# Turning the second unit's wide loads without a regrouping copy, first loads from two queues, a small mask pattern, and a new order

## The chip, the core and the metric

The kernel runs on one core of one Trainium2 chip. The metric is the device time of one execution in microseconds (us). Three executions of the kernel before took 289.61, 290.24 and 291.42 us; the median is 290.24. Engines are named as in the profile: PE is TensorE, ACT is ScalarE, DVE is VectorE, POOL is GpSimd, SP is SyncE. SP only issues transfers here.

## What is computed

Chunk-selected causal attention on 4 batches, 8 heads, 768 positions of 64 elements, followed by a gated feed-forward layer on 3072 tokens of 512 elements with a hidden width of 1536. All inputs and the output are fp32.

```python
k_chunks = k.reshape(B, H, nc, chunk, D)            # nc = 24 chunks of 32 keys
k_min, k_max = k_chunks.min(axis=3), k_chunks.max(axis=3)
ub = sum over d of max(q * k_min, q * k_max)        # an upper bound per query and chunk
top_chunks = argsort(where(causal, ub, -1e9))[..., -6:]
scores = where(chunk in top_chunks and causal, q @ k.T / sqrt(D), -1e9)
x = softmax(scores) @ v                             # heads side by side: 3072 x 512
return (sigmoid(x @ w_gate) * (x @ w_val)) @ w_out
```

## The kernel before

The 3072 tokens are cut into eight units, u0 to u7, of 384 tokens or less: three blocks of 128 positions each. u0 holds the first blocks of batches 0, 1 and 2, in which every causal key is selected (at most four chunks), so that it needs no choice. u1 holds blocks 1 to 3 of batch 0, u2 blocks 4 and 5 of batch 0 and the first block of batch 3, and so on. Each unit is attended, and then goes through the feed-forward layer; u4 with u5 and u6 with u7 go through it in pairs, with seven block products in place of eight.

Every piece of work is added to a plan with `plan.add` (lines 49 to 72): a name, the engines that may do it, what it reads and writes. The order of all pieces, the engine of each and the slot of each buffer are written out in the string `ORDER` (lines 94 to 254): `kn_u1_3@POOL:1` means that the piece `kn_u1_3` goes to POOL and its new buffer takes slot 1 of its kind. The first engine in a piece's list is taken where `ORDER` names none. Each engine, and each queue of transfers, runs its pieces strictly in that order.

The names that matter here:

- `kf0_b`, `kf1_b`, `qf0_b`, `qf1_b`, `vf_b` (lines 514 to 528): the loads of u0 for batch b; k and q in two halves of 4 heads, each 128 x 4 rows of 256 bytes (512 rows), v in one load of 1024 such rows. They are issued on SP.
- `k0_u1` to `k3_u1`, `q0_u1` to `q3_u1` (`load_wide`, lines 530 to 539): the wide loads of u1, two heads each, 256 rows of 768 bytes; those of u2 are 256 rows of 512 bytes. In them one partition holds three consecutive positions (x) of each head. They are issued on SP.
- `kn_u1_p`, `qn_u1_p` (`turned`, lines 684 to 698): a copy [128, 384] fp32 on ACT, DVE or POOL that brings the two heads of one position side by side. Then `kT_u1_p`, `qT_u1_p`: three PE transpositions of 128 x 128 fp32 through `ident32` into PSUM.
- `kt_`, `hk0_`, `hk1_`, `kx0_`, `kx1_`, `kcr_` for keys, `qf_`, `qm_`, `hq0_`, `hq1_` for queries: casts, reductions and copies of what was turned. `ub_u1` are the bound products, which need all four `qf_u1`, all four `qm_u1` and `kcr_u1`. `ubn`, `mx`, `ap`, `apt`, `hqm` make the choice from them.
- for u0 and each batch b: `kfT_b`, `qfT_b` (transpositions), `kf16_b`, `qf16_b` (casts), `scm_b` (the causal mask, added by a product), `scf_b` (scores), `expf_b_e`, `pvf_b_e`, `rzf_b_e`, `xf_b_e`, `xpsf_b_e`, `xTf_b_e`. When the last `xTf` is done, `g_u0_0` starts, the first product of the feed-forward layer (line 940).
- `epat0` and `epat` (lines 454 to 462): a mask pattern [64, 2, 24, 32] in fp16, cleared by DVE and filled on POOL by two selections of 32 x 768. `hkp...` (line 476) copy it eight times to the upper or lower halves of the key tiles.
- `ident` (POOL) and `ident16` (DVE, its fp16 cast); `wm_0` to `wm_23` are 24 products without use, which keep PE busy.
- `wg0`, `wv0` to `wg2`, `wv2`, `wo0` to `wo2`: the weights, issued by POOL, which converts them to fp16 on the way. `wg0` and `wv0` come behind `after0` and the others behind `after1` (lines 493 to 511): copies of one word on POOL that wait for the load of `qf1_1` and of `qf1_2`.

ACT runs no transfers before. Its first instruction is the load of the activation table, its second `kn_u1_1`.

Of the kernel before, what the change touches and what calls it, by code (L numbers as in the profile page):

```python
# [94 lines left out]
k3_u1:0 epat0:0 k1_u1 tri0 epat k0_u1 q1_u1 q3_u1 q2_u2:1 hkp100@POOL kf1_0:0 qf0_0:1 kn_u1_1:0 kf0_0 hkp111@ACT ident  # L95
qf1_1:2 hkp010@POOL ident16 hkp011 wm_0:0 k2_u1 kT_u1_1:1 q3_u2 kn_u1_3@POOL:1 wm_1 q2_u1 kt_u1_1:0 wm_2 kcr0
qn_u1_3:2 k2_u2 qn_u1_1@DVE:3 v10 qf1_0 qT_u1_3:2 kx0_u1_1 vf_0:3 hkp110 wm_3 after0 qf_u1_3:0 qf0_1 kx1_u1_1:0 wm_4
tri kn_u1_0:4 kn_u1_2@POOL:5 wm_5 qn_u2_3@DVE:6 kT_u1_0:3 wm_6 kf0_1:4 kT_u1_3:4 kt_u1_0:1 kx1_u1_0 wm_7 q1_u2
qm_u1_3@ACT:0 kfT_0:5 kx1_u1_3 kf1_1 wm_8 hk0_u1_0 wm_9 kxf0 vf_1:5 hkp101 q0_u2 v16_0_0 kf16_0@DVE:0 qf1_2:0
hk0_u1_1@POOL kx0_u1_0 qfT_0:6 wm_10 wm_11 qf16_0:2 wm_12 scm_0:7,2 kt_u1_3:2 wm_13 scf_0:1 kT_u1_2:1 kn_u2_2@POOL:4  # L100
kx0_u1_3 kf0_2:1 expf_0_1:2 wm_14 kT_u2_2:6 kxf1:1 kf1_2 expf_0_0 scm_1:3,4 q0_u1 hkp001 qn_u2_1:1 qT_u1_1:2 hq0_u1_3
pvf_0_1:5 qf0_2 rzf_0_1:0 kcr_f qf_u1_1@DVE kfT_1:7 k3_u2 kf16_1:2 qT_u2_1:2 vf_2:3 hq1_u1_3 after1 pvf_0_0:7
hk1_u1_0@POOL wm_15 k0_u2 rzf_0_0:1 qm_u1_1@ACT kx1_u2_2:1 wg0 qf_u2_1:1 kx0_u1_2 qfT_1:2 kx1_u1_2 wv0 k1_u2 wm_16
xf_0_0:0 v_0_3:4 qf16_1:5 hk1_u1_3 qn_u1_2@POOL:4 v_0_1:2 qn_u1_0@DVE:3 kt_u1_2:1 scf_1:3 kfT_2:7 vf1_2:1 expf_1_0
kx0_u2_2 vf1_1:2 qT_u1_2:2 vc_1 hq1 kf16_2:5 qT_u1_0:1 ap0 wm_17 wv1 xf_0_1:1 qf_u1_2 pvf_1_0:3 qfT_2:7 qf_u1_0@DVE
expf_1_1:1 v_0_2:1 scm_2:5,2 ap1 qm_u1_2@ACT qm_u1_0@POOL wm_18 qf16_2@DVE:4 hk1_u1_1@ACT pvf_1_1:1 wm_19 kcr_u1@POOL
xpsf_0_0:4,0 qn_u2_0:3 rzf_1_1:0 wm_20 kn_u2_3@POOL:2 xf_1_1:2 scf_2:2 hkf1 kt_u2_2@DVE:0 xpsf_1_1:7 expf_2_1:3
xpsf_0_1:1 rzf_1_0:0 xf_1_0:0 hq0_u1_2@POOL hq0_u1_0 ub_u1:6,2 kcr1 wg1 xTf_0_0@ACT vc_2@ACT qn_u2_2@POOL:4 hkp000@ACT
kn_u2_0@DVE:5 wg2 pvf_2_1:3 wm_21 rzf_2_1:0 qT_u2_3:4 xTf_1_1 wm_22 ubn0_u1:0 hq1_u1_0@POOL xf_2_1:2 expf_2_0 ubm0_u1
wv2 qf_u2_3@DVE hkf0@ACT pvf_2_0:7 qT_u2_0:6 hq1_u1_1@POOL rzf_2_0:0 xpsf_1_0:3 xTf_0_1@ACT xpsf_2_1:4 xf_2_0:1 wm_23  # L110
xTf_1_0@ACT hk0_u1_2@POOL qT_u2_2:0 hq0 kn_u2_1:0 ubn1_u1 wo1 xTf_2_1@ACT xpsf_2_0:5 xTf_2_0 kT_u2_3:1 k10_1:0
mx0_u1:0 g_u0_0:7,0,0 hk1_u1_2@POOL ap0_u1 wo0 v_u0_0:3 ubm1_u1 kt_u2_3@DVE:1 apt0_u1:0 g_u0_1:2,1,1 hq1_u2_1@POOL
hqm0_u1_2@ACT hqm0_u1_0 v_u0_1:4 tanh_u0_1 g_u0_2:5,2,2 hk0_u1_3@POOL tanh_u0_0 hg_u0_1 qm_u2_3@POOL:0 qf_u2_2
sc_u1_3_0:2,1 hg_u0_0 tanh_u0_2 sc_u1_0_0:7,3 sc_u1_3_1:4 qf_u2_0 v_u0_2:0 hq1_u1_2@DVE exp_u1_0_0 kx1_u2_3 kT_u2_1:5
qm_u2_0@ACT sc_u1_0_1:3 kT_u2_0:6 kx0_u2_1 exp_u1_0_1 sc_u1_3_2:7 mx1_u1 exp_u1_3_2 g_u0_3:3,3,3 exp_u1_3_0
hq0_u2_1@DVE sc_u1_2_0:7,0 hq0_u2_0@DVE cm_u1_3 v_0_4:5 tanh_u0_3 v_u0_3:2 kx0_u2_3 exp_u1_3_1 hg_u0_2 hq0_u1_1@POOL
sc_u1_2_1:3 exp_u1_2_0 g_u0_4:1,1,4 kx1_u2_1 v16_0_3 hk1_u2_3@ACT hg_u0_3 v_u0_4:4 ap1_u1 tanh_u0_4 g_u0_5:0,0,5
hg_u0_4 v_u0_5:7 apt1_u1 tanh_u0_5 kx0_u2_0 hqm1_u1_2 exp_u1_2_1 sc_u1_2_2:2 hqm1_u1_0@DVE sc_u1_1_0:1,2 g_u0_6:4,2,6
cm_u1_0 hq0_u2_2@DVE sc_u1_1_1:0 v_u0_6:3 tanh_u0_6 v11 exp_u1_1_0 kx1_u2_0 g_u0_7:4,3,7 hq1_u2_3@POOL hg_u0_6
kt_u2_1:2 qm_u2_1@ACT cm_u1_1 v_u0_7:1 hg_u0_5 hq1_u2_0@POOL kcr_u2 sc_u1_0_2:5 wo2 exp_u1_0_2 sc_u1_1_2:3  # L120
g_u0_8:7,1,8 exp_u1_1_2 hq0_u2_3 v16_0_1 v_u0_8:5 exp_u1_1_1 cm_u1_2 tanh_u0_8 g_u0_9:3,2,9 hk1_u2_1@POOL qm_u2_2@ACT
tanh_u0_7 v_u0_9:0 exp_u1_2_2 hg_u0_7 g_u0_10:7,0,10 hk0_u2_1 ub_u2:4,2 tanh_u0_10 kt_u2_0:2 hk1_u2_2@ACT v_u0_10:1
tanh_u0_9 g_u0_11:7,3,11 v16_0_2 hg_u0_10 v_u0_11:6 ubn0_u2:0 tanh_u0_11 k11_1 hg_u0_8 pv_u1_3:3 hg_u0_9 pv_u1_1:1
pv_u1_2 hg_u0_11 sc_u1_7_1:4,1 sc_u1_7_2:7 rz_u1_1:0 pv_u1_0 sc_u1_4_1:5,3 rz_u1_0:1 exp_u1_4_1 sc_u1_5_1:0,2
o0_u0_0:6,0 x_u1_0:0 exp_u1_5_1 mx0_u2:0 exp_u1_7_1 sc_u1_4_2:5 sc_u1_4_0:1 ubn1_u2 exp_u1_4_0 sc_u1_7_0:0 k01_1
ap0_u2 x_u1_1:2 exp_u1_7_0 sc_u1_6_1:4,0 o1_u0_0 apt0_u2:0 exp_u1_4_2 xps_u1_0:2,1 cm_u1_7 mx1_u2 xps_u1_1:1
exp_u1_7_2 sc_u1_6_2:3 xT_u1_0@ACT sc_u1_5_0:0 cm_u1_4 hk1_u2_0 exp_u1_5_0 sc_u1_5_2:5 o2_u0_0 hqm0_u2_0 exp_u1_6_1
o0_u0_1:7,1 hqm0_u2_2@ACT cm_u1_5 osb_u0_0@DVE vf1_3:6 exp_u1_5_2 ap1_u2 sc_u1_6_0:2 out_u0_0 hk0_u2_3@ACT hk0_u2_2
pv_u1_4:0 pv_u1_5 exp_u1_6_0 sc_u2_3_0:4,3 rz_u1_2:0 sc_u2_3_1:6 apt1_u2 o1_u0_1 k00_1 x_u1_2:1 exp_u2_3_1 hqm1_u2_2
q00_1:1 exp_u1_6_2 pv_u1_7:5 cm_u1_6 exp_u2_3_0 sc_u2_7_1:2,1 xps_u1_2:0 sc_u2_3_2:6 cm_u2_3 pv_u1_6 xT_u1_2  # L130
exp_u2_3_2 o2_u0_1 rz_u1_3:0 xT_u1_1@ACT x_u1_3:0 hqm1_u2_0@DVE sc_u2_7_0:3 o0_u0_2:4,0 hk0_u2_0 q10_1 xps_u1_3:0
o1_u0_2 xT_u1_3@ACT exp_u2_7_0 sc_u2_4_0:6,2 o2_u0_2 k16_1_0@ACT:1 kx0_1_1 k16_1_2:3 v_0_5:0 exp_u2_7_1 v16_0_4
g_u1_0:1,0,12 kx1_1_3:1 osb_u0_2 k16_1_3:4 v_u1_0:5 tanh_u1_0 kx0_1_2 exp_u2_4_0 g_u1_1:0,1,13 cm_u2_7 hq1_u2_2
kt_1_0:2 qf1_3:3 sc_u2_4_1:3 sc_u2_1_0:2,0 v_u1_1:4 q11_1 exp_u2_1_0 kt_1_3:0 q01_1 tanh_u1_1 g_u1_2:1,2,14 cm_u2_1
osb_u0_1 kt_1_2:5 sc_u2_1_2:6 sc_u2_7_2:2 v_u1_2:0 exp_u2_7_2 hk0_1_0@DVE tanh_u1_2 sc_u2_1_1:7 hg_u1_1 v16_0_5
g_u1_3:2,3,15 exp_u2_1_2 hg_u1_0 hk1_1_2@ACT cm_u2_4 v_u1_3:1 kx1_1_1 out_u0_2 exp_u2_1_1 g_u1_4:4,1,16 kx1_1_0
sc_u2_4_2:6 pv_u2_1:5 tanh_u1_4 v_u1_4:7 kx0_1_3 exp_u2_4_2 k16_1_1@ACT:1 out_u0_1 hg_u1_2 g_u1_5:4,0,17 tanh_u1_3
v_1_1:4 v_u1_5:6 kx1_1_2 tanh_u1_5 kf1_3:2 exp_u2_4_1 g_u1_6:0,2,1 qf0_3 hg_u1_4 v_u1_6:2 hg_u1_3 tanh_u1_6 kx0_1_0
pv_u2_3:4 g_u1_7:3,1,0 hg_u1_6 k01_2:0 sc_u2_2_2:7,3 sc_u2_0_0:1,0 qf0_u4_0:0 v_u1_7:0 v_1_0:1 kcr_1 exp_u2_0_0
qf0_u3_1:1 sc_u2_2_0:2 tanh_u1_7 qf0_u3_0 g_u1_8:1,3,2 v16_1_1 exp_u2_2_2 qf0_u3_2 exp_u2_2_0 sc_u2_2_1:3 hg_u1_5  # L140
v_u1_8:7 qm_u3_0@ACT:0 cm_u2_2 qf0_u3_3 g_u1_9:2,2,3 k00_2 cm_u2_0 tanh_u1_8 qf0_u4_2 hg_u1_7 sc_u2_0_1:6 k11_2
tanh_u1_9 v_u1_9:1 hg_u1_8 exp_u2_2_1 sc_u2_0_2:0 qm_u3_2 g_u1_10:2,0,4 hq0_u3_0@ACT kt_1_1:3 pv_u2_2 exp_u2_0_1
v_u1_10:7 qf0_u4_3 exp_u2_0_2 v16_1_0 hk0_1_1@DVE ub_u3:3,6 tanh_u1_10 k10_2 hk1_1_1 hk0_1_3@ACT sc_u2_6_1:0,3
hq0_u3_2@POOL ubn1_u3:0 pv_u2_0 g_u1_11:2,1,6 rz_u2_1:0 ubn0_u3 hk1_1_3 vf_3:5 rz_u2_0:1 qf0_u4_1 v_u1_11:6 tanh_u1_11
# [5 lines left out]
x_u2_2:0 hqm0_u3_2@ACT rz_u2_3:0 kx0_2_3 cm_u3_1 qfT_3:5 v16_1_3 kfT_3:1 x_u2_3:1 q11_2 qf16_3:5 hq1_u3_0@POOL  # L150
sc_u3_6_0:0,2 xT_u2_0 sc_u3_0_0:4,0 exp_u3_1_2 xps_u2_3:3 o2_u1_1 kf16_3:3 xT_u2_3 v16_1_2 kx1_2_3:1 exp_u3_0_0
xps_u2_2:2 sc_u3_0_2:5 cm_u3_0 xT_u2_2@ACT kt_2_2:0 exp_u3_6_0 scf_3:7,3,3 o0_u1_2:1,0 q00_2 exp_u3_0_2 kx1_2_2
sc_u3_0_1:4 expf_3_0 pv_u3_1:2 xps_u2_1:0 o1_u1_2 expf_3_1:1 cmf_3_0 kx0_2_0 exp_u3_0_1 cmf_3_1 pvf_3_0:5 xT_u2_1@ACT
# [142 lines left out]
def kernel(  # L296
# [159 lines left out]
    def pattern(e):  # L456
        for i in range(2):
            t = at(epat)[32 * i:32 * i + 32, i]
            nc.gpsimd.affine_select(out=t, in_=t, compare_op=ALU.not_equal, fill=NEG, base=0,
                                    pattern=[[-1, NC], [0, CH]], channel_multiplier=1)  # L460
# [776 lines left out]
```

## Time and profile before

| | |
|---|---|
| Median of three runs | 290.24 us (289.61 to 291.42) |
| The profiled execution's own time | 291.67 us |
| Its span, first to last instruction | 290.0 us |
| First matmul (`wm_0`) | starts at 7.50 us |
| `g_u0_0`, the first feed-forward product | starts at 34.40 us |
| PE busy before / from 34.4 us on | 22.75 of 34.40 us / 251.3 of 255.6 us |
| First-loads: bytes (u0, u1, u2) | 2.36 + 1.57 + 1.05 MB |

All times below are us from the span's start. "Busy" on PE counts a matmul from its start to the modelled end; matmuls overlap. PEclk is the granted TensorE clock as a share of full speed. In the DMA views, q1 is the queue of transfers issued by SP, q0 that of POOL; a row gives packets, MB, and the time that the packets took as a share of the 16 DMA engines' time. MB are counted at the destination.

### The profile page before, as it was taken

What the parts mean: (1) busy time and instruction counts of PE and PEld (TensorE: products, weight loads), DVE (VectorE), ACT (ScalarE), POOL (GpSimd) and SP (SyncE); (2) the same over time, 40 slices, a digit from 0 to 9 for tenths busy, and PEclk for the clock granted to TensorE, in tenths of its full rate; (3) what the DMA queues carried; (4) which work ended last, traced back from release to release, by engine and by line L of the source; (5) the groups of instructions that cost most, each with busy time, mean ns of one, the idle gap of its engine ahead of it and who ended that gap; (6) DMA issues with size and microseconds to landing.
All of it is one profiled execution on the core that took longest, in us unless ns stands there. A gap on an engine that the chain in (4) does not pass through costs nothing.

```text
span 290.0 us, 7126 instructions
## 1 busy us (share of the span) xinstructions
PE 274.1 (95%) x2650; PEld 174.3 (60%) x2650; DVE 233.0 (80%) x642; ACT 215.2 (74%) x457; POOL 112.4 (39%) x180
## 2 busy tenths in 40 slices
PE   0979799999999999999999999999999999999994
...
GB/s 185 239 242 185 204 203 192 157 157 184 217 177 171 212 181 167 219 203 193 175 40 1 3 38 38 73 5 0 0 3 0 75 72 38 36 1 2 1 106 113
DMA packets 123379, 32.71 MB, mean 113 GB/s; under 512 B 111440, under 2 KB 120400, under 8 KB 123344
## 3 DMA queue, kind: packets, MB, share of 16 engines
...
HBM read 30.67 MB, written 6.29 MB: 127 GB/s over the span
## 4 chain that ended last, share of the span: by engine, by line
PE 82%; ACT 10%; DVE 4%; POOL 1%; issue 1%; ACTq 0%; POOLq 0%; DVEq 0%
PE o_u L971 21%; PE sc_u L857 11%; PE g_u L940 10%; PE v_u L940 10%; PE pv_u L890 7%; PE ube_u L796 2%; PE sug_u6u L1049 2%; PE suv_u6u L1049 2%; ACT gate_u4u L1074 2%; PE suv_u4u L1049 2%; PE xps_u L917 1%; PE srg_u6u L1049 1%; PE sug_u4u L1049 1%; PE spare L1136 1%; PE srv_u6u L1049 1%
## 5 line engine op out<-in xcount | busy, mean ns | idle before, releaser
L868 ACT ACTIVATE att_u<-sc_u 128x512 f16<-128x512 f32 (+3 forms) x184 | 91.4, 554 | 15.3 <-PE sc_u L857 14.6
L874 POOL TENSOR_SCALAR_AFFINE_SELECT att_u<-att_u 128x384 f16<-128x384 f16 (+1 forms) x56 | 29.6, 536 | 77.9 <-ACT att_u L868 72.8
L971 PE MATMUL o_u<-wo,hg_u 128*128 128x512 f16 x216 | 53.6, 379 | 0.0
L940 PE MATMUL g_u<-xT_u,wg 128*128 128x384 f16 x192 | 39.0, 326 | 0.5 <-ACT att_u L868 0.3
L940 PE MATMUL v_u<-xT_u,wv 128*128 128x384 f16 x192 | 39.0, 326 | 0.0
L952 DVE SCALAR_TENSOR_TENSOR hg_u<-gate_u,v_u 128x384 f16<-128x384 f16 x48 | 24.8, 534 | 8.3 <-ACT gate_u L948 4.5
L971 PEld LDWEIGHTS <-hg_u 128*128 128x128 f16 x216 | 19.8, 98 | 17.1
L948 ACT ACTIVATE gate_u<-g_u 128x384 f16<-128x384 f32 x48 | 23.1, 490 | 8.5 <-PE g_u L940 7.1
L857 PE MATMUL sc_u<-hqe,hke 128*128 128x128 f16 (+2 forms) x220 | 28.9, 243 | 0.0
L890 PEld LDWEIGHTS <-att_u 128*128 128x128 f16 x640 | 25.1, 97 | 4.7 <-issue 0.6
L857 PE MATMUL sc_u<-hqo,hko 128*128 128x128 f16 (+2 forms) x220 | 27.4, 243 | 0.0
L890 PE MATMUL pv_u<-v,att_u 128*128 128x65 f16 x640 | 27.2, 193 | 0.0
L940 PEld LDWEIGHTS <-wg 128*128 128x128 f16 x192 | 18.1, 98 | 11.7 <-issue 1.1
L940 PEld LDWEIGHTS <-wv 128*128 128x128 f16 x192 | 18.2, 98 | 10.6 <-issue 0.4
L857 PEld LDWEIGHTS <-hko 128*128 128x128 f16 x220 | 16.6, 98 | 7.3 <-issue 0.9
L857 PEld LDWEIGHTS <-hke 128*128 128x128 f16 x220 | 17.0, 98 | 6.3 <-issue 0.6
L980 ACT ACTIVATE osb_u<-o_u 128x512 f32<-128x512 f32 (+1 forms) x16 | 9.4, 596 | 11.6 <-PE o_u L971 11.6
L562 POOL CAST v<-v 128x512 f16<-128x512 f32 x23 | 13.9, 611 | 8.7 <-DMA v<-in_v_dram 8.3
L1136 PE MATMUL spare<-ident 128*128 128x512 f16 x24 | 9.7, 452 | 7.5 <-DVE ident L480 7.5
L971 PE MATMUL o_u<-wo,hgp_u 128*128 128x512 f16 (+1 forms) x72 | 16.4, 370 | 0.0
L909 DVE TENSOR_TENSOR x_u<-pv_u,rz_u 128x384 f16<-128x384 f32 (+1 forms) x28 | 14.7, 529 | 0.6 <-DVE rz_u L907 0.2
L1049 PEld LDWEIGHTS <-Sv 128*128 128x128 f16 x96 | 9.1, 98 | 6.2 <-issue 0.3
(225 smaller groups left out, 609.2 us busy)
## 6 DMA issues: line engine op xcount, KB each, us to landing
...
```

Of the source, the lines that this page charges most:

```text
L562: plan.add(f"v16_{b}_{ib}", {POOL: pool(H * D)}, lambda e: nc.gpsimd.tensor_copy(v16[b % 2][:, ib, :, 0:D], at(t)), reads=[t], writes=[("v ...
L857: nc.tensor.matmul(at(t)[:, o:o + 128 * m], hk[b % 2][e_][:, p, 128 * jb:128 * jb + 128], hq[u.side][e_][:, p, 128 * x:128 * (x + m)], sta ...
L868: plan.add(f"exp_{u.name}_{h}_{y}", {ACT: act(n)}, lambda e, t=t, att=att, b0=b0, n=n: nc.scalar.activation(at(att)[:, b0:b0 + n], at(t), ...
L874: nc.gpsimd.affine_select(out=dv, in_=dv, compare_op=ALU.is_ge, fill=0.0, base=0, pattern=[[0, u.m], [1, 128]], channel_multiplier=-1)
L890: nc.tensor.matmul(at(pv)[:, last, x, :], at(att)[:, c:c + 128], v16[b % 2][:, jb, h, :], start=(jb == 0), stop=(jb == ib))
L909: plan.add(f"x_{u.name}_{p}", {DVE: dve(u.t)}, lambda e: nc.vector.tensor_tensor(at(x_).rearrange("p a (e d) -> p e a d", e=2), at(pv)[:, ...
L940: nc.tensor.matmul(at(t), w16[:, c, 128 * fb:128 * fb + 128], at(u.xt)[:, c, :], start=(c == 0), stop=(c == 3))
L948: plan.add(f"tanh_{u.name}_{fb}", {ACT: act(T)}, lambda e, g=g, gate=gate: nc.scalar.activation(at(gate), at(g), AF.Tanh, scale=0.5), read ...
L952: plan.add(f"hg_{u.name}_{fb}", {DVE: dve(T)}, lambda e, w_=w_, gate=gate, hg=hg: nc.vector.scalar_tensor_tensor(at(hg), at(gate), 1.0, at ...
L971: nc.tensor.matmul(at(o), hgs[c][1][1]()[:, 128 * tb:128 * tb + 128], wo16[:, fc, lo:hi], start=(c == 0), stop=(c == NFB - 1))
L1049: nc.tensor.matmul(at(t), left[i](c), right[i](c), start=first and c == 0, stop=c == 1, skip_group_check=not first)
L1136: plan.add(f"wm_{i}", pe(512 / 2.4 + 2.4), lambda e: nc.tensor.matmul(at(spare), ident16, ident16.unsqueeze(1).to_broadcast([128, 4, 128]) ...
```

## The change

1. `turned`: for u1 alone there is no `kn_u1_p` or `qn_u1_p` (eight copies fewer). For each position PE now takes the first head (128 x 64, fp32) by a transposition into PSUM rows 0 to 63, and the second by a product with `ident32` into rows 64 to 127: 24 transpositions and 24 fp32 products in place of 24 transpositions. u2 is turned as before.
2. Loads `kf`, `qf`, `vf`, `k_u1`, `q_u1`, `k_u2`, `q_u2` and `v_0_*` may be issued by SP or ACT. `ORDER` gives ACT 14 of them ahead of everything else on ACT, the activation table's load among it, three more after `kt_u1_1`, one before the last `xTf`, and one later.
3. The pattern is made as [64, 2, 24] (cleared by DVE, two selections of 32 x 24 on POOL), and spread by two copies to 64 x 768, `epat0` and `epat1`, on DVE.
4. `ORDER` is written anew from the first word to the last, engines and slots included.

```diff
-    const("epat0", {DVE: (480, 560)}, lambda e: nc.vector.memset(at(epat), 0.0), writes=[epat], prio=-3)
+    pat = lone("pat", [64, 2, NC])
+    const("pat0", {DVE: (70, 80)}, lambda e: nc.vector.memset(pat, 0.0), writes=["pat"], prio=-3)
...
+    for o in range(2):
+        const(f"epat{o}", {POOL: pool(S), DVE: dve(S, 1, 64), ACT: act(S, False, 64)}, lambda e, o=o: copy(
+            e, at(epat)[:, o], pat[:, o].unsqueeze(2).to_broadcast([64, NC, CH])),
+            reads=["pat"], writes=[(epat, o)], prio=-2.3)
...
-                plan.add(f"{'kq'[j]}{p}_{u.name}", {SP: (450, 450)}, lambda e, j=j, p=p, src=src: nc.sync.dma_start(
+                plan.add(f"{'kq'[j]}{p}_{u.name}", {SP: (450, 450), ACT: (450, 450)}, lambda e, j=j, p=p, src=src: (
+                    nc.scalar if e == ACT else nc.sync).dma_start(
...
+        straight = u.i in (1,)
+        if not straight:
+            nat = Buf("np", f"{n}n_{u.name}_{p}", [128, m, 2, D])
...
+                if straight:
+                    nc.tensor.transpose(at(t)[ROWS[0], x:u.t:m], at(u.raw)[:, j, p, 0, x], ident32)
+                    nc.tensor.matmul(at(t)[ROWS[1], x:u.t:m], at(u.raw)[:, j, p, 1, x], ident32, start=True, stop=True)
```

The head of the new `ORDER`, with what stands on ACT and POOL up to the first weights:

```
vf1_2:0 k1_u1@ACT:0 kf0_0:0 v10 pat0 tri0 ident qf1_0@ACT:1 qf0_0 pat ident16 kf1_0@ACT qf1_1:2 tri epat0@DVE:0 wm_0:0
q1_u1@ACT vf1_1:1 q3_u1 scm_0:1,2 qf0_1@ACT qf0_2:3 hkp000 kf0_1@ACT:4 vf_0:5 wm_1 epat1@DVE kf1_1@ACT wm_2 k3_u1 wm_3
hkp011 hkp101@POOL q2_u2@ACT:1 kT_u1_1:3 kcr0 qf1_2@ACT hkp001 q2_u1@ACT hkp100@POOL kfT_0:4 q0_u1 wm_4 wm_5
kf16_0@DVE:2 kf1_2:0 qT_u1_1:5 k2_u1@ACT k3_u2 kxf1:0 k0_u1@ACT wm_6 kxf0 k0_u2@ACT qfT_0:6 wm_7 vf_2@ACT:1
qf16_0@DVE:3 qfT_1:7 qf16_1@DVE:4 kfT_1:4 v16_0_0 vf_1:4 hkf1@DVE kf0_2 qf_u1_1:0 qT_u1_3:6 kx1_u1_1:1 scf_0:1
expf_0_0 kf16_1@DVE:5 kT_u1_3:7 after1 hkp111@POOL hq0_u1_1 qf_u1_3@DVE q3_u2 qfT_2:5 expf_0_1:2 kt_u1_3@DVE:0
scm_1:1,4 kt_u1_1:1 qf16_2@DVE:6 pvf_0_0:6 hk1_u1_3@POOL q0_u2@ACT kT_u1_2:2 rzf_0_0:0 k1_u2 kx1_u1_3 after0 k2_u2@ACT
wg0 xf_0_0:0 v_0_3:5 q1_u2@ACT wm_8 kx1_u1_2 wv0 v_0_2:3 kt_u1_2:2 kx0_u1_3 kT_u1_0:5 hk0_u1_3@ACT qm_u1_1@POOL:0
```

The PE pieces from there to `g_u0_0` in the new order:

```
wm_8 kT_u1_0 scf_1 wm_9 wm_10 wm_11 pvf_0_1 qT_u1_2 xpsf_0_0 wm_12 kfT_2 wm_13 qT_u1_0 pvf_1_0 scm_2 scf_2 kT_u2_3
wm_14 xpsf_1_0 wm_15 wm_16 pvf_2_1 qT_u2_2 wm_17 pvf_2_0 pvf_1_1 xpsf_0_1 wm_18 ub_u1 xpsf_2_0 wm_19 wm_20 xpsf_1_1
wm_21 kT_u2_0 wm_22 xpsf_2_1 kT_u2_1 qT_u2_3 g_u0_0
```

The order's end: before it is `osb_u7_0 out_u7_0` (a copy of 128x512 and its store), after it is `osbb_u7_2 outb_u7_2` (128x128).

380 lines of the change are left out of this document (189 added, 191 removed).

## The prediction

> **What bounds the kernel now.** I read the page first: the busy line, the slices and the shares of the chain that ended last.
>
> ```profile
> span 290.0 us, 7126 instructions
> PE 274.1 (95%) x2650; PEld 174.3 (60%) x2650; DVE 233.0 (80%) x642; ACT 215.2 (74%) x457; POOL 112.4 (39%) x180
> ...
> PE   0979799999999999999999999999999999999994
> ...
> PE 82%; ACT 10%; DVE 4%; POOL 1%; issue 1%; ACTq 0%; POOLq 0%; DVEq 0%
> ```
>
> PE is busy 95% of the span, and its slices have room only at the two ends. So the kernel is a head, in which PE waits, and a long stretch in which PE is the limit. Where the head ends is seen in the table of windows (columns: length, then busy us and count of PE, PEld, DVE, ACT, POOL; granted clock, DMA share, GB/s), cut at the first product of the feed-forward layer:
>
> ```profile
> 0.00:34.40 34.40, 22.75 (x182) 14.61 (x183) 22.41 (x59) 20.32 (x39) 21.46 (x41) 0.95 1.01 212
> 34.40:68.10 33.70, 33.42 (x316) 21.35 (x317) 24.16 (x89) 24.28 (x58) 16.88 (x32) 1.00 1.15 176
> 68.10:104.10 36.00, 36.00 (x374) 23.54 (x372) 32.34 (x86) 30.43 (x63) 14.10 (x24) 1.00 1.07 195
> ...
> 247.00:290.00 43.00, 39.09 (x227) 21.42 (x225) 31.19 (x64) 22.82 (x52) 0.00 (x0) 0.99 0.12 44
> ```
>
> Before 34.4 PE idles 11.65 us. From there on it idles 0.3 us up to 68 and 3.9 us at the very end. What the change can win or lose is therefore the start of `g_u0_0`, plus what PE work crosses that point, plus the last microseconds. Next the timeline of the head and the tail:
>
> ```profile
> 0.79 1.28 ACT L345 ACT_TABLE_LOAD   x1 [0.79 <-PEq L1221]
> ...
> 1.78 2.02 POOL L459 TENSOR_SCALAR_AFFINE_SELECT epat<-epat 32x768 f16<-32x768 f16 x2 [1.28 <-DVE tri L485]
> ...
> 3.88 0.51 ACT L345 COPY kn_u<-kq_u 128x384 f32<-128x384 f32 x1 [1.80 <-DMA kq_u<-in_k_dram]
> ...
> 7.50 0.61 PE L1136 MATMUL spare<-ident 128*128 128x512 f16 x1 [7.50 <-DVE ident L480]
> ```
>
> ```profile
> 18.54 0.18 POOL L496 COPY word<-qf 1x1 f32<-1x1 f32 x1 [3.18 <-DMA qf<-in_q_dram]
> 18.78 0.51 POOL L349 COPY hko<-kt_u 64x384 f16<-64x384 f16 x1
> 19.23 0.99 POOL L501 DMA_DIRECT2D wg<-in_moe_w_gate_dram  x1
> ```
>
> ```profile
> 31.61 0.60 ACT L650 ACTIVATE attf<-scf 128x512 f16<-128x512 f32 x1
> ...
> 34.40 0.81 PE L940 MATMUL g_u<-xT_u,wg 128*128 128x384 f16 x4 [0.25 <-DVE xT_u L347]
> ```
>
> PE starts late because POOL fills the pattern and copies it before it makes `ident`. Yet that start is not what sets 34.4: the end of the head is batch 2 of u0, whose last exponential ends on ACT at 32.2, and from it 2.2 us of `pvf`, `xf`, `xpsf` and `xTf` lead to `g_u0_0`. Last, the transfers by queue, each view over one window (2 to 8, 8 to 14, 14 to 19, then 22 to 26 and 26 to 30 us):
>
> ```profile
> q1 hardware_dynamic: 3223, 1.50, 95.2%
> ```
> ```profile
> q1 hardware_dynamic: 4124, 1.42, 95.9%
> ```
> ```profile
> q1 hardware_dynamic: 3965, 1.18, 103.6%
> ```
> ```profile
> q0 software_dynamic: 535, 0.54, 89.8%
> q1 hardware_dynamic: 442, 0.16, 20.6%
> ```
> ```profile
> q0 software_dynamic: 615, 0.61, 90.2%
> q1 hardware_dynamic: 623, 0.16, 29.8%
> ```
>
> One queue alone keeps the engines 95 to 104% busy from 2 us on, at 0.250, 0.237 and 0.236 MB/us. Once the weights flow, both queues move about as many packets (535 and 442, 615 and 623), and the loads fall to 0.04 MB/us. A weight packet takes 0.898 x 64/535 = 107 ns of an engine, a 256-byte load packet some 30 ns (0.206 x 64/442).
>
> **The change, part by part.**
>
> *The mask pattern and the early PE start.* 2.02 us on POOL and a DVE memset go; two copies of 64 x 768 come, between the copies of 64 x 384 (0.26 us) and of 64 x 1536 (0.85 us at most) that I see on DVE, so 0.5 to 1.7 us, I take 1.1. `ident` no longer stands behind them, and PE starts near 2.5 us instead of 7.5. On the end this is worth nothing by itself: the first data that PE can use land at 3.9 us (`kn_u1_1` above), and the loads go on until about 20.
>
> *Eight copies less.* At 0.51 us (row above) about 4.1 us go, three each from ACT and POOL and two from DVE. None is on the path to the last `xTf`; they shorten queues.
>
> *24 products of fp32.* The row nearest is the transposition of the same 128 columns, three in 0.49 us; the upper bound comes from the bound products, 32 records (four groups like the one below) in 1.7 us (28.54 to 30.28), 54 ns for 320 columns with up to eight side by side, 430 ns for one alone, 172 ns for 128 columns, two records for each fp32 product: 344 ns.
>
> ```profile
> 18.16 0.49 PE L695 MATMUL qT_u<-ident,qn_u 128*128 128x128 f32 x3
> ```
> ```profile
> L796 PE MATMUL ube_u<-qf_u,kcr x8: 429/441/453, 28.5 to 29.3; 64*32 64x320 f32 x8
> ```
>
> So 3.9 to 8.3 us of PE, all of it before `g_u0_0`, in the 11.65 idle us. I take 0.25 us each. Near the end of the head only `qT_u1_0` (three) stands between `kfT_2` and `scf_2`, and it runs beside the cast `kf16_2`. If that cover is gone it costs 0.5 to 1.0 us.
>
> *Two queues.* The DMA rows say that the loads are limited by the engines, not by the issue; so two queues do not bring them earlier as a whole. They do three other things. First, ACT now issues 14 transfers before its table load. One issue takes 0.49 us where the queue is free and more where it is full:
>
> ```profile
> 0.79 1.46 SPq L536 DMA_DIRECT2D kq_u<-in_k_dram  x3
> ...
> 5.47 1.37 SPq L525 DMA_DIRECT2D qf<-in_q_dram  x1
> ...
> 11.05 1.45 SPq L525 DMA_DIRECT2D kf<-in_k_dram  x1
> ```
> ```profile
> q1 hardware_dynamic: 6095, 2.61, 81.1%
> ```
>
> The second fence is the queue from 0 to 12.5 us, where the issue at 11.05 came free: 7168 packets (rows) had been issued and 6095 moved, so a queue holds about 1,100. ACT's 14 transfers are 5888 packets; the last is through when some 4,800 of them have moved. With the two queues in turn, packet by packet, 3840 of each have moved at 12.9 us (2.69 MB at the rates above), and the next 960 of ACT, three quarters of them of 768 bytes, with as many of SP, are about 0.9 MB more: 16.5 us. Then the table, 1.28: 17.8. From there to the last `xTf` ACT has 26 instructions (mean 0.52 us: 20.32 over 39 in the window of the head) and four issues: 13.5 + 2.0. The floor by ACT alone is 33.3 us. The low end is an ACT that isn't held (14 x 0.49 + 0.79 + 1.28, free at 8.9: floor 24.4).
>
> Second, the order of landing. `kf0_2`, the last key load of u0, is number 12 on SP, packet 6144 of that queue.
>
> Third, the weights. In the new order `wg0` stands on POOL behind `after1`, `hkp111`, `hk1_u1_3`, `after0`. `qf1_2` is packet 3840 on ACT's queue: landed at 13.2. Then 0.2 to 0.5 for the word, 1.46 for `hkp111` (row below), 0.51, again 0.2 to 0.5: `wg0` is issued at 15.8, not 19.23. Its packets flow about 2.7 us later (19.23 to 22 before): 18.5. By then SP's queue has moved some 5,420 packets (12.9 us + 1.33 MB: 768 of each queue, then 256, then 555), so that 725 remain to `kf0_2`, 45 on each engine. In turn with one weight packet and one of ACT's queue, 107 + 30 + 30 ns each: 7.6 us, `kf0_2` lands at 26.1. Without weights it would be 20.1.
>
> The Trainium skill, page "DMA: Bandwidth & Descriptors", section "Issuing engines are not separate DMA queues", says that transfers started by several engines run on the same 16 DMA engines, and that issuing from several saves only the sequencer's time. By that rule this part brings no load earlier and its sum is the stalls on ACT alone; the 95% of the first window agrees, and issue time saved is worth nothing where the issues of 1.37 and 1.45 us already wait for the engines.
>
> ```profile
> 3.87 1.46 POOL L349 COPY hke<-epat 64x1536 f16<-64x1536 f16 x1
> ```
> ```profile
> 24.40 0.58 ACT L345 CAST kf<-kfT 128x512 f16<-128x512 f32 x1 [0.53 <-PE kfT L598]
> ...
> 33.41 0.41 PE L695 MATMUL qT_u<-ident,qn_u 128*128 128x128 f32 x2
> ```
>
> *From there to `g_u0_0`.* ACT reaches `kf16_2` at 27.2 (17.8 + 15 instructions and three issues up to `vc_2`, 7.8 + 1.5), so it ends at 27.8, 1.0 after `kfT_2` could have allowed. Then `pvf_1_0`, `scm_2`, `scf_2` 0.9; two `expf` 1.2; `pvf_2_0` 0.3: 30.2. Behind it PE's queue still has the rest of the list in the order: `ub_u1` 1.7 us, three transpositions of u2 at 0.4, five `wm` at 0.22, `pvf_1_1` and four `xpsf` 0.6: 4.6 us. `g_u0_0` starts at 34.8 to 35.1; I take 35.0. In the order before, `ub_u1` was done at 30.3, ahead of the last `expf`.
>
> *Across that point and at the end.* One `wm` (0.22) and one transposition of u2 (0.41) more come after `g_u0_0`: +0.6. The last copy was 128 x 512 and is 128 x 128:
>
> ```profile
> 281.06 0.29 DVE L981 TENSOR_SCALAR osb_u<-ob_u 128x128 f32<-128x128 f32 x1
> ...
> 286.17 0.60 ACT L980 ACTIVATE osb_u<-o_u 128x512 f32<-128x512 f32 x1 [5.08 <-PE o_u L971]
> ```
>
> That is -0.3, and a store of a quarter of the bytes, which I put at -0.2: -0.5. The stretch between has no idle time to win; a new order can shift it by a microsecond or so either way.
>
> **The sum**: (35.0 - 34.4) + 0.6 - 0.5 = +0.7 us. On the profiled execution (span 290.0, 291.67 in all) that is a span of 290.7; on the median, 290.24, it is 290.9. No change that a measurement can tell: 1% (2.9 us) is about what this kernel's runs can tell from none.
>
> **The rivals.**
>
> *Slower: the loads of u0 are caught by the weights.* Place: `kf0_2`. If the two queues of loads together get one turn in two, the 725 packets of each take 91 x 137 ns = 12.4 us: landing at 30.9, then `kfT_2` and `kf16_2` 1.3, the same 2.4 to `pvf_2_0` and 4.6: `g_u0_0` near 39.3, +4.9 + 0.1, 295.2 us. It decides once `kf0_2` lands after 29 us (37.3 for `g_u0_0`). For it: 0.04 MB/us beside the weights. Against: the counts 535 to 442 and 615 to 623 are shares by queue, whatever the size of a packet. Chance 0.25. The Trainium skill, the same page, section "Queues, rings and completion order", says that each engine goes round the queues that have work; by that SP's and ACT's queues would have a turn each, and the landing would be 26.1, not 30.9; no row of before has two queues of loads.
>
> *Faster: ACT isn't held and the weights come late.* If a second queue takes its transfers at 0.49 us each and the loads are down by 20.1, the chain behind is 1.3 + 2.4 + 4.6 and `g_u0_0` starts at 28.4 to 29: 285.0 us. With only one of the two, ACT's floor or the landing still gives 33.5 or so, 289.3. Against: the 1.37 and 1.45 us issues. Chance 0.19.
>
> *The clock.* The granted clock fell after PE had been busy two thirds of the time:
>
> ```profile
> 20.00:22.00 2.00, 1.42 (x12) 0.84 (x12) 1.50 (x5) 1.19 (x3) 1.56 (x4) 1.00 1.18 241
> 22.00:24.00 2.00, 1.49 (x13) 1.24 (x13) 1.91 (x7) 1.56 (x3) 0.61 (x3) 0.63 1.02 162
> 24.00:26.00 2.00, 2.00 (x14) 1.66 (x12) 0.65 (x2) 1.60 (x4) 0.72 (x2) 0.52 1.18 188
> ```
>
> If PE waits for `kf0_2` or ACT around 26 and the clock is halved over the 4.6 us list, +2.3: 293.2, the upper end of the likeliest case. The Trainium skill, "TensorE: Matmul & The Clock Gate", Part 1, puts the drop behind an idle window of some 3.4 us; the row shows the drop, not its cause.
>
> **How the numbers follow.** The forecast holds 0.56, with 289.3 to 293.2 as its own range; slower by the weights 0.25, faster 0.19. The range reaches into both: 286.5 to 295.5. Faster by over 1%: 0.18, from the second rival. Slower: 0.30, the first and 0.05 of the forecast's upper end. Within 1%: 0.52.
>
> **What would show it.** The first matmul near 2.5 us; ACT's table load near 16.5 us and SP's and ACT's issues with stalls; `wg0` issued near 15.8; `kfT_2` at 26 or later; `ub_u1` behind the last `expf`; `g_u0_0` at 35.0. I am wrong if ACT's table load starts before 10 us, if `kfT_2` starts before 22, or if PE idles more than a microsecond after `g_u0_0`.

## The result and the profile after

Four executions of the changed kernel, measured beside the kernel before on one chip, took 291.77 to 294.88 us, median 293.79; the kernel before took 290.05 there. The ratio is 1.0103, with a 95% interval of 1.006 to 1.0146: about 3 us slower. A second series (below) gives 292.64 us and 1.010 (1.0063 to 1.0136). The profiled execution took 293.53 us, its span is 291.8. From its page, the rows that answer to those of before:

```profile
span 291.8 us, 7194 instructions
PE 284.5 (97%) x2698; PEld 177.4 (61%) x2698; DVE 237.9 (82%) x650; ACT 206.3 (71%) x440; POOL 116.2 (40%) x183
...
PE   6999999999999999999999999999999999999995
...
PE 84%; DVE 6%; DMA 4%; POOL 2%; ACT 2%; issue 1%; SPq 0%; DVEq 0%; POOLq 0%; ACTq 0%
```

PE has 10.4 us more work, and the holes in its first slices are gone. The table of windows, cut at `g_u0_0`:

```profile
0.00:34.84 34.84, 32.28 (x228) 17.21 (x229) 21.75 (x56) 12.73 (x27) 22.94 (x42) 1.00 1.17 224
34.84:68.00 33.16, 33.00 (x322) 21.51 (x320) 25.98 (x96) 25.75 (x61) 11.86 (x20) 1.00 1.02 165
68.00:104.00 36.00, 35.39 (x358) 22.64 (x357) 32.91 (x82) 26.30 (x55) 22.93 (x37) 1.00 1.03 183
...
288.40:291.80 3.40, 0.00 (x0) 0.00 (x0) 0.00 (x0) 0.24 (x1) 0.00 (x0) 0.91 0.28 96
```

Up to `g_u0_0` PE is now busy 32.28 of 34.84 us, where it was 22.75 of 34.40: the head has become PE's. Behind it PE idles 0.6 us between 68 and 104, where it had no idle time. The timeline, PE first, then ACT, POOL and SP:

```profile
1.93 0.61 PE L1154 MATMUL spare<-ident 128*128 128x512 f16 x1 [1.93 <-DVE ident L487]
...
9.05 1.06 PE L1154 MATMUL spare<-ident 128*128 128x512 f16 x2
...
10.87 0.42 PE L709 MATMUL qT_u<-ident,kq_u 128*64 128x128 f32 x1
...
11.62 0.30 PE L709 MATMUL qT_u<-ident,kq_u 128*64 128x128 f32 x1
...
18.87 0.27 PE L709 MATMUL kT_u<-ident,kq_u 128*64 128x128 f32 x1
19.08 0.43 PE L710 MATMUL kT_u<-ident,kq_u 128*64 128x128 f32 x2
19.44 0.30 PE L709 MATMUL kT_u<-ident,kq_u 128*64 128x128 f32 x1
...
25.82 0.60 PE L609 MATMUL kfT<-ident,kf 128*128 128x128 f32 x4
...
34.84 0.81 PE L958 MATMUL g_u<-xT_u,wg 128*128 128x384 f16 x4
```
```profile
13.61 1.28 ACT L347 ACT_TABLE_LOAD   x1 [13.61 <-DMA kq_u<-in_q_dram]
```
```profile
18.62 0.50 POOL L351 COPY hko<-kt_u 64x384 f16<-64x384 f16 x1 [3.86 <-DVE kt_u L349]
...
19.30 1.00 POOL L508 DMA_DIRECT2D wg<-in_moe_w_gate_dram  x1
```
```profile
14.79 0.58 SPq L534 DMA_DIRECT2D kf<-in_k_dram  x1
```

One pair of a transposition (L709) and a product (L710, two records each) takes 0.57 us from start to start (18.87 to 19.44), 24 times; before PE's full pace it takes 0.97. `kfT_2` starts at 25.82 with no wait shown: it stood in PE's queue, and its data were long there (`kf0_2`, the SP row, was issued at 14.79, and such loads landed at most 5.4 us after their issue, so by 21). `g_u0_0` is at 34.84 us, near the 35.0 of the forecast, but not for its reasons: that agreement is luck.

### The profile page after: what moved, and what is told of

Same layout as the page of the kernel before. It is cut to its first block, busy times and chain, and to the rows that moved or that the text cites. A ratio compares the mean times of both kernels' runs of the same rounds, so it can differ in the third digit from the quotient of the medians.

```text
span 291.8 us, 7194 instructions
## 1 busy us (share of the span) xinstructions
PE 284.5 (97%) x2698; PEld 177.4 (61%) x2698; DVE 237.9 (82%) x650; ACT 206.3 (71%) x440; POOL 116.2 (40%) x183
## 4 chain that ended last, share of the span: by engine, by line
PE 84%; DVE 6%; DMA 4%; POOL 2%; ACT 2%; issue 1%; SPq 0%; DVEq 0%; POOLq 0%; ACTq 0%
PE o_u L989 18%; PE sc_u L875 10%; PE v_u L958 8%; PE g_u L958 8%; PE pv_u L908 6%; PE sug_u6u L1067 3%; PE suv_u4u L1067 3%; PE suv_u6u L1067 3%; PE sug_u4u L1067 3%; PE spare L1154 2%; PE ube_u L814 2%; DMA k<-in_k_dram 2%; DMA kf<-in_k_dram 2%; PE kT_u L710 2%; PE qT_u L710 2%
## 5 line engine op out<-in xcount | busy, mean ns | idle before, releaser
L966 ACT ACTIVATE gate_u<-g_u 128x384 f16<-128x384 f32 x48 | 23.1, 493 | 10.3 <-PE g_u L958 9.9
L875 PE MATMUL sc_u<-hqo,hko 128*128 128x128 f16 (+2 forms) x220 | 28.5, 243 | 0.0
L908 PE MATMUL pv_u<-v,att_u 128*128 128x65 f16 x640 | 27.8, 193 | 0.1
L989 PE MATMUL o_u<-wo,hgp_u 128*128 128x512 f16 (+1 forms) x72 | 16.5, 370 | 0.0
L573 POOL CAST v<-v 128x512 f16<-128x512 f32 x23 | 15.2, 665 | 1.5 <-DMA v<-in_v_dram 1.5
L998 ACT ACTIVATE osb_u<-o_u 128x512 f32<-128x512 f32 x15 | 8.9, 599 | 9.8 <-PE o_u L989 9.3
L597 POOL TENSOR_SCALAR qm_u<-qf_u 128x320 f32<-128x320 f32 (+2 forms) x5 | 8.3, 1665 | 10.9 <-DVE qf_u L781 4.5
L837 DVE MAX8 mx_u<-ubn_u 128x8 f32<-128x8 f32 (+16 forms) x152 | 12.5, 157 | 0.1
```

Source lines behind the costliest of these rows:

```text
L573: plan.add(f"v16_{b}_{ib}", {POOL: pool(H * D)}, lambda e: nc.gpsimd.tensor_copy(v16[b % 2][:, ib, :, 0:D], at(t)), reads=[t], writes=[("v ...
L837: nc.vector.max(at(mx)[:, e_, j, :], at(ubn)[:, e_, j, 0:max(8, u.seen[j])])
L875: nc.tensor.matmul(at(t)[:, o:o + 128 * m], hk[b % 2][e_][:, p, 128 * jb:128 * jb + 128], hq[u.side][e_][:, p, 128 * x:128 * (x + m)], sta ...
L908: nc.tensor.matmul(at(pv)[:, last, x, :], at(att)[:, c:c + 128], v16[b % 2][:, jb, h, :], start=(jb == 0), stop=(jb == ib))
L966: plan.add(f"tanh_{u.name}_{fb}", {ACT: act(T)}, lambda e, g=g, gate=gate: nc.scalar.activation(at(gate), at(g), AF.Tanh, scale=0.5), read ...
L989: nc.tensor.matmul(at(o), hgs[c][1][1]()[:, 128 * tb:128 * tb + 128], wo16[:, fc, lo:hi], start=(c == 0), stop=(c == NFB - 1))
```

## The experiments

Four theories were held against each other. T1: the products fill PE and so set the head's end. T2: ACT, held to 13.6 us by the transfers it issues, sets it. T3: the loss lies behind `g_u0_0`, in the new order. T4, formed after four runs (products alone, copies back, one queue, fewer spare products): behind `g_u0_0` the new order has a second floor (a limit that shows once the head is shorter), DVE waiting for k_2 to land. Each ratio is to the kernel before in the same series of runs (medians 290.05, 290.00 and 290.14 us).

**The two kernels once more.** First, since all else is read against them. No edit.

> The kernel before once more, one look: its profile fell on an execution with the clock at 0.63 and 0.52 in 22 to 26 us (290.0 us of span), and most of its runs have a span near 288.2. Without the drop I expect g_u0_0 at 32.4 to 33.0 us and the same 255.6 us behind it.

> The changed kernel once more, for the spread. The profiles so far show PE's products at half pace until about 7 us in some executions (head loads on SP, fewer spare products) and until 11.4 us in others (the profile of the changed kernel). If that is what splits the times, they fall in two groups near 291.8 and near 294, with g_u0_0 near 33.3 where the pace rises early and 34.8 where it rises late, and the loads' second queue is worth nothing either way. If the second queue costs 1.4 us, all times lie above those of the kernel with the head's loads on SP (292.2 to 294.0).

Before: 289.71 us. Changed: 291.52, 291.65, 293.63 and 293.73 us, so two groups as expected; the profile is of the one at 291.65. The windows of both (head, rest of PE's work, tail), before and changed:

```profile
0.00:32.28 32.28, 20.95 (x182) 13.06 (x183) 21.88 (x59) 20.22 (x39) 21.43 (x41) 1.00 1.08 216
32.28:284.10 251.82, 251.33 (x2468) 159.72 (x2468) 210.55 (x586) 194.34 (x417) 91.30 (x140) 1.00 0.52 100
284.10:287.90 3.80, 0.00 (x0) 0.00 (x0) 0.00 (x0) 0.60 (x1) 0.00 (x0) 0.98 0.32 113
```
```profile
0.00:33.03 33.03, 30.47 (x228) 16.38 (x229) 21.68 (x56) 12.62 (x27) 22.89 (x42) 1.00 1.15 223
33.03:286.50 253.47, 252.13 (x2473) 160.18 (x2470) 215.83 (x596) 193.21 (x414) 92.54 (x141) 1.00 0.51 99
286.50:289.90 3.40, 0.00 (x0) 0.00 (x0) 0.00 (x0) 0.26 (x1) 0.00 (x0) 1.00 0.28 96
```

Without the fall of the clock that the first profile of before had at 22 to 26 us, `g_u0_0` is at 32.28, not 34.40 (just under the 32.4 to 33.0 expected, with the same 255.6 us behind it), and the span 287.9, not 290.0. Other executions agree: over the three series, 13 of the kernel before have a mean granted clock of 0.992, as that first profile has, and took 290.91 to 291.73 us; the other 46, at 0.997 or more, took 289.44 to 290.81. Against it the changed kernel's 289.9 is +2.0: head +0.75, work behind it +0.80, idle time behind it +0.85 (1.34 against 0.49), tail -0.4. In the changed kernel's first profile the head takes 1.8 us more. PE's work in the second:

```profile
6.19 0.42 PE L709 MATMUL kT_u<-ident,kq_u 128*64 128x128 f32 x1
...
6.95 0.30 PE L709 MATMUL kT_u<-ident,kq_u 128*64 128x128 f32 x1
...
8.04 0.59 PE L1154 MATMUL spare<-ident 128*128 128x512 f16 x2
```

This is the pair of spare products that took 1.06 us at 9.05 in the first profile. In both executions PE starts at a lower pace; a lone transposition falls from 0.42 to 0.30 us at about 7 us here, and at about 11.4 there. With a head full of PE work the difference shows in full.

**Products alone.** The kernel before with the new `turned`, and its eight copies struck from `ORDER`.

```diff
-k1_u1 ... kn_u1_1:0 kf0_0 hkp111@ACT ... kT_u1_1:1 q3_u2 kn_u1_3@POOL:1 ...
+k1_u1 ... kf0_0 hkp111@ACT ... kT_u1_1:1 q3_u2 ...
```

> The kernel before, with only the eight copies replaced by 24 pairs of transposition and product, in the old order; one queue, the large pattern and the late PE start (7.5 us) stay. T1 (the price of the products, 0.59 us a pair against 0.16 for the transposition it replaces, fills PE in the head): PE's work in the head grows from 22.75 by about 10 to 33 us, and g_u0_0 moves from 34.4 to 38 to 41; the time is 294 to 297 us. T2 (ACT held by its issues) and T3 (the order of the dense part): the products lie in PE's idle time, g_u0_0 at 34 to 35, 289 to 291 us; the stretch behind g_u0_0 is 251.8 as before under T3 and T1 alike.

302.29 us, ratio 1.0394 (1.0352 to 1.0437). The head:

```profile
0.00:44.57 44.57, 33.64 (x230) 17.34 (x231) 21.01 (x57) 19.09 (x36) 19.27 (x38) 1.00 0.84 176
```

PE's work up to `g_u0_0` rises from 20.95 to 33.64 us, and `g_u0_0` moves by 12.3: PE's idle time stays (10.93 of 44.57 against 11.33 of 32.28), so hardly any of the products went into it. Of the 11.33 us, 7.50 lie ahead of PE's first matmul, which waits for `ident`, as any product would. Of the 12.7 us of added work some 2.3 are there because six pairs run before PE's full pace, at 0.97 us each. This is T1's sign, and more than T1 had asked for (38 to 41 for `g_u0_0`, 294 to 297 us).

**Copies back.** The changed kernel without the products.

```diff
-        straight = u.i in (1,)
+        straight = False
...
-... wm_3 hkp011 hkp101@POOL q2_u2@ACT:1 kT_u1_1:3 ...
+... wm_3 hkp011 hkp101@POOL q2_u2@ACT:1 kn_u1_1@DVE:2 kT_u1_1:3 ...
```

(and seven more such words: one on DVE, two on POOL, four on ACT; `vf1_2` and `vc_2` behind `qT_u1_0`.)

> The changed kernel with the eight copies and the plain transpositions back for the second unit (two copies on DVE, two on POOL, four on ACT), all else as changed. T1: PE's work up to g_u0_0 falls from 32.3 to about 22 us and something else ends the head: g_u0_0 between 28 and 32.5, 288 to 291.5 us. T2: ACT is held to 13.6 us as before and has four copies more, so g_u0_0 is at 34.8 or later, 293.5 to 295.5 us. T3: the loss is behind g_u0_0, which stays near 34.8 whatever the head does: 293 to 294 us, with 253.5 us from g_u0_0 to PE's end.

292.53 us, ratio 1.0079 (1.0058 to 1.0099). Windows, and PE's wait between 34 and 110 us:

```profile
0.00:32.22 32.22, 22.66 (x180) 13.24 (x181) 23.12 (x58) 14.19 (x31) 22.49 (x42) 1.00 1.13 222
...
68.00:104.00 36.00, 34.29 (x359) 22.07 (x358) 31.58 (x81) 27.19 (x57) 22.63 (x37) 1.00 1.03 187
```
```profile
PE o_u L990 <- DVE x_u L928: 1.4, 1, 1.4
```

Against the changed kernel's first profile, in which PE comes to its full pace about as late as here (four transpositions take 1.06 us at 10.59 and 0.60 at 12.36), PE's work in the head falls by 9.6 us, `g_u0_0` comes 2.6 us earlier, and the span is only 0.9 shorter (290.9). Most of the rest is given back behind it: PE idles 1.7 us between 68 and 104 instead of 0.6. Against the execution with the early pace (33.03 and 289.9) the head is 0.8 us shorter and the span 1.0 longer. So T1's `g_u0_0` came (28 to 32.5) and its time (288 to 291.5) did not, and the ratio, 1.0079, is not clear of the changed kernel's 1.0103 and 1.010. And the head at 32.22 is no earlier than before's 32.28, although PE starts 5.6 us sooner: without the products something else ends it.

**One queue.** All 25 loads of ACT back on SP: 17 of the head, `v_0_1`, and seven later ones (the list under The change counts one of these seven).

```diff
-vf1_2:0 k1_u1@ACT:0 kf0_0:0 v10 pat0 tri0 ident qf1_0@ACT:1 ... v_0_1@ACT:2 ...
+vf1_2:0 k1_u1:0 kf0_0:0 v10 pat0 tri0 ident qf1_0:1 ... v_0_1:2 ...
```

> The changed kernel with all 25 of ACT's loads back on SP, products and order kept. T1: ACT is free from 2 us on, but PE's queue is full from the time its data land, so g_u0_0 stays at 34 to 36.5 and the time at 293 to 295.5 us. T2: ACT's table load goes from 13.6 to about 1 us and g_u0_0 comes two or more us earlier, 289 to 292 us. T3: nothing changes, 293 to 294 us.

299.85 us, ratio 1.0313 (1.026 to 1.0366), which no theory had. `g_u0_0` is at 33.00; the loss is later. PE, POOL and SP around it:

```profile
54.23 0.62 PE L907 MATMUL pv_u<-v,att_u 128*128 128x65 f16 x8 [5.90 <-POOL att_u L891]
```
```profile
53.09 0.61 POOL L572 CAST v<-v 128x512 f16<-128x512 f32 x1 [5.88 <-DMA v<-in_v_dram]
```
```profile
26.49 5.78 SPq L555 DMA_DIRECT2D k<-in_k_dram  x1
32.37 15.92 SPq L566 DMA_DIRECT2D v<-in_v_dram  x1
```

`v_0_1` now stands on SP behind `k10_1`, whose 128-byte rows fill the queue; its issue is held for 15.92 us and it lands at 53. POOL's cast waits for it, the piece of `att_u1` behind that cast on POOL waits too, and `pv_u1` waits 5.9 us. That is most of the 8.0 us between this span, 297.9, and 289.9; PE waits 1.4 us more later, and the granted clock is 0.90 between 33 and 68. In time the run measures the place of one load, not T2. So the head alone was undone next.

**Head loads on SP.** Only the first 17 loads back on SP; `v_0_1` and later ones stay on ACT.

```diff
-vf1_2:0 k1_u1@ACT:0 kf0_0:0 v10 pat0 tri0 ident qf1_0@ACT:1 ... q1_u2@ACT ... v_0_1@ACT:2 ...
+vf1_2:0 k1_u1:0 kf0_0:0 v10 pat0 tri0 ident qf1_0:1 ... q1_u2 ... v_0_1@ACT:2 ...
```

> The changed kernel with only the 17 loads of the head back on SP; the later loads (v_0_1 and behind) stay on ACT, so that none of them stands behind the 128-byte transfers of k_1. If the 6 us of the one-queue run came from v_0_1 behind k_1, PE does not idle for 5.9 us at 48 us, and g_u0_0 is at 33.0 as there: T2 (ACT held is the loss) gives 291 to 292.3 us. If the 1.8 us that the head gains are given back at a later floor: 292.5 to 294 us. If two queues do bring the loads earlier: over 295 us.

292.35 us, ratio 1.0091 (1.006 to 1.0123). ACT's table load, and the head:

```profile
0.79 1.28 ACT L346 ACT_TABLE_LOAD   x1 [0.79 <-PEq L1238]
```
```profile
0.00:33.39 33.39, 30.58 (x227) 16.44 (x228) 21.67 (x56) 12.71 (x27) 22.88 (x42) 1.00 1.05 215
```

ACT is free at 2 us instead of 14.9, and the head is as long as in the changed kernel with the full pace at 7 us (33.39 against 33.03; span 290.3 against 289.9). The five times, 292.19 to 294.0, lie among the changed kernel's (291.52 to 294.88). The median falls between two of the ranges set (to 292.3, and from 292.5), so the time decides nothing; the head does. T2 falls; the second queue is worth nothing in the head that these runs can tell.

**Fewer spare products.** The changed kernel without `wm_4` to `wm_22`, 19 products that compute nothing.

```diff
-    for i in range(24):
+    for i in [0, 1, 2, 3, 23]:
```

> The changed kernel without 19 of the 24 spare products (numbers 4 to 22), which compute nothing that is stored; at 0.22 us each they are 4.2 us of PE's work in the head. T1: PE is what bounds the head, so most of the 4.2 us comes off: g_u0_0 at 30.5 to 32.5, 289.5 to 291.5 us. T2 and T3: spare products cost nothing, g_u0_0 at 34.3 to 35, 293 to 294 us. If PE then idles and the granted clock falls, the time is up to 2 us longer than T1 says.

294.21 us, ratio 1.0097 (1.0062 to 1.0133): ten executions in two groups, four at 291.45 to 291.75 and six at 294.2 to 294.87. The profiled one (291.65) has the full pace at 7 us, and is compared with the changed kernel's 289.9 of the same kind. Windows, PE's waits, and DVE:

```profile
0.00:31.05 31.05, 27.30 (x209) 14.89 (x210) 21.24 (x53) 12.47 (x28) 22.48 (x42) 1.00 1.14 223
...
68.00:104.00 36.00, 33.78 (x355) 21.93 (x354) 30.76 (x82) 26.90 (x56) 22.44 (x37) 1.00 0.98 173
```
```profile
PE pv_u L907 <- POOL att_u L891: 1.4, 1, 1.4
PE o_u L988 <- DVE x_u L926: 0.6, 1, 0.6
```
```profile
92.45 0.98 DVE L580 TRANSPOSE_TENSOR_REDUCE kcr<-k 128x24 f32<-128x768 f32 x1 [2.81 <-DMA k<-in_k_dram]
```

`g_u0_0` comes 2.0 us earlier (31.05 against 33.03), so PE does set the head's end there; the span is 289.9 as without the edit, and the time that T1 gave (289.5 to 291.5) did not come. Nearly all of it is given back between 68 and 104, where PE idles 2.2 us instead of 0.6.

**The reduction later.** The same, with `kx0_2_0` (the DVE row above) moved behind `x_u2_2`, which it had held up.

```diff
-... exp_u2_5_2 kx0_2_0 o2_u1_0 ... exp_u3_0_1 x_u2_2:2 cm_u3_1 ...
+... exp_u2_5_2 o2_u1_0 ... exp_u3_0_1 x_u2_2:2 kx0_2_0 cm_u3_1 ...
```

> The changed kernel without the 19 spare products, as in the run before, and with one reduction of k_2 (kx0_2_0, on which DVE waits at 92.5 us for k_2 to land) moved in the order to stand behind x_u2_2. T4 (the second floor is DVE waiting for k_2, with x_u2 queued behind it): PE's wait of 0.6 us for x_u goes and the levels fall by 0.5 to 1.5 us against that run: 290 to 293.5 us, median below 293.5. Rival: the floor is the landing of the loads as a whole (v_0_5 before it, 1.4 us), and the time stays at 291.5 to 294.5 us.

291.78 us, ratio 1.007 (1.0037 to 1.0103).

```profile
68.00:104.00 36.00, 34.71 (x363) 22.66 (x362) 31.80 (x83) 27.90 (x58) 22.67 (x37) 1.00 0.98 180
```

PE regains 0.9 of the 2.2 us, and the profiled span is 289.0. But not where the edit acts. PE's waits here, then POOL's cast of a piece of v in the run before and in this one:

```profile
PE pv_u L907 <- POOL att_u L891: 0.5, 1, 0.5
PE sc_u L874 <- POOL hqo L350: 0.5, 1, 0.5
PE pv_u L907 <- POOL v L572: 0.3, 1, 0.3
```
```profile
83.69 0.61 POOL L572 CAST v<-v 128x512 f16<-128x512 f32 x1 [1.49 <-DMA v<-in_v_dram]
```
```profile
82.75 0.61 POOL L572 CAST v<-v 128x512 f16<-128x512 f32 x1 [0.62 <-DMA v<-in_v_dram]
```

The wait for `x_u` is gone, as T4 asked. Yet others take its place, and from 90 to 104 PE idles 0.76 us against 0.84. The gain is the wait of `pv_u` at 87 to 88 us (0.5 for 1.4), ahead of the moved reduction: in this execution v landed 0.9 us sooner. That speaks for the rival, the landing of the loads as a whole; that k_2 by itself is a floor is not shown. Group by group (six at 290.69 to 291.89, four at 293.2 to 294.39) the times fell by 0.3 to 0.7 us in the mean, with no cause shown; the medians, which differ by more because the groups are of other sizes, lie in the ranges of both.

**Neither products nor spare products.** Both edits together.

```diff
-        straight = u.i in (1,)
+        straight = False
...
-    for i in range(24):
+    for i in [0, 1, 2, 3, 23]:
```

> The changed kernel with the copies back and without the 19 spare products: PE's work up to g_u0_0 is some 18 us. T1: PE no longer bounds the head; ACT (held to 13.8 us) and the loads do, g_u0_0 at 30 to 32 us. If a second floor behind g_u0_0 holds (T4), the time is that of either run alone: 290.5 to 293 us. If only the head counted, it would be 287 to 289 us. A fall of the granted clock in PE's idle time would add up to 2 us.

291.85 us, ratio 1.0047 (1.0026 to 1.0068).

```profile
0.00:31.69 31.69, 22.76 (x160) 14.78 (x161) 23.21 (x55) 14.20 (x32) 21.64 (x40) 0.84 1.14 222
```

PE idles 8.9 us in the head, and the granted clock is 0.84 there. The time is 0.7 us below that of the copies back and 2.4 below that of fewer spare products, in T4's range and not in 287 to 289. From 68 to 104 PE idles 1.95 us. The second floor holds, whatever it is made of, though the fall of the clock may have taken a part of the gain; how much was not measured.

**Old order behind.** The changed kernel up to `g_u0_0`, then what is left in the order of before, slots assigned anew.

```diff
-... mx0_u1:0 qn_u2_0:3 g_u0_0:2,0,0 hq0_u1_2@POOL ubn1_u1 hk1_u1_1@POOL ...
+... mx0_u1:0 qn_u2_0:3 ... hq1_u1_1@POOL wm_23 ubn1_u1 g_u0_0:6,0,0 ap0_u1 v_u0_0:2 ubm1_u1 ...
```

> The changed kernel up to g_u0_0 (its loads, products and order), and from there the operations that are left in the order of the kernel before, with slots assigned anew. T3 (the new order behind g_u0_0 costs 1 to 2 us of PE work and waits): from g_u0_0 to PE's end 251.8 us instead of 253.5, 290.5 to 292.5 us. T1 (all that is lost is the head's): 293 to 294.5 us, since the head is kept.

291.74 us, ratio 1.0058 (1.0036 to 1.0079).

```profile
0.00:34.77 34.77, 31.60 (x235) 17.06 (x236) 23.36 (x66) 13.76 (x31) 25.04 (x44) 1.00 1.16 222
34.77:286.30 251.53, 251.03 (x2464) 159.14 (x2463) 210.38 (x581) 194.41 (x418) 87.64 (x135) 1.00 0.50 98
```

Behind `g_u0_0` it is before's stretch again, 251.5 us with 0.5 idle, 1.9 less than the changed kernel. But what the old order had done ahead of `g_u0_0` came to stand there, with 1.1 us more PE work, and the head grew by 1.7; the span is 290.1. PE's waits in the new order behind do go (none between 68 and 104, where the changed kernel has 0.6 us), and the longer head takes back what that gives. The time was inside T3's range, and yet like is like here (full pace at 7 us in both): 290.1 against 289.9. T3 as stated falls: with this head, changing the order behind `g_u0_0` gains nothing.

**Small pattern alone.** The kernel before with part 3 of the change; `ident` right behind `pat`, `epat0` and `epat1` on DVE.

```diff
-k3_u1:0 epat0:0 k1_u1 tri0 epat k0_u1 q1_u1 ... kf0_0 hkp111@ACT ident qf1_1:2 ...
+k3_u1:0 pat0 k1_u1 tri0 pat ident epat0@DVE:0 epat1@DVE k0_u1 q1_u1 ... kf0_0 hkp111@ACT qf1_1:2 ...
```

> The kernel before with the small mask pattern alone (filled as 64 x 2 x 24, spread by two copies on DVE; the identity made right behind it); loads, copies, transpositions and the rest of the order as before. The first matmul moves from 7.5 to about 3 us. If the early start is worth nothing (my step), g_u0_0 stays at 33 to 34.4 and the time at 289 to 291 us. Rival: PE's late start is what makes the head long, as the products' alone run suggests (it lost all of their 10 us); then up to 4 us come off, 286 to 288 us.

289.12 us, ratio 0.9966 (0.9951 to 0.9981): 0.3% below the kernel before.

```profile
2.99 0.61 PE L1142 MATMUL spare<-ident 128*128 128x512 f16 x1 [2.99 <-DVE ident L486]
```
```profile
0.00:31.54 31.54, 23.02 (x182) 14.25 (x183) 22.10 (x61) 20.21 (x39) 19.79 (x41) 1.00 1.06 216
```

PE starts 4.5 us sooner, and the head ends 0.7 us sooner: the start is not what sets it there, as the forecast had it, but it is worth a little. (The 33 to 34.4 expected for `g_u0_0` came from the profile with the fall of the clock.)

**Masks on DVE.** The same, with `hkp000` and `hkp111` moved from ACT to DVE, behind `kcr0`.

```diff
-... kf0_0 hkp111@ACT qf1_1:2 ... wm_2 kcr0 qn_u1_3:2 ... vc_2@ACT qn_u2_2@POOL:4 hkp000@ACT kn_u2_0@DVE:5 ...
+... kf0_0 qf1_1:2 ... wm_2 kcr0 hkp000@DVE hkp111@DVE qn_u1_3:2 ... vc_2@ACT qn_u2_2@POOL:4 kn_u2_0@DVE:5 ...
```

> The kernel before with the small mask pattern, and with two of the mask copies (hkp000 and hkp111, 1.47 us each on ACT, one of them right ahead of u0's last exponential) moved to DVE, which idles at 4.9 to 6.5 us. If ACT ends the head there, the last exponential starts 1.2 to 1.5 us earlier, g_u0_0 is at 29.8 to 30.5 us and the time at 287.5 to 288.3 us, below both kernels. If the head's gain is given back behind g_u0_0 as in the new order: 288.7 to 289.5 us.

288.51 us, ratio 0.9938 (0.9916 to 0.9961), the best of all. u0's last exponential without and with the move, then a wait of PE's that is new:

```profile
28.75 0.60 ACT L656 ACTIVATE attf<-scf 128x512 f16<-128x512 f32 x1
```
```profile
27.00 0.59 ACT L656 ACTIVATE attf<-scf 128x512 f16<-128x512 f32 x1
```
```profile
PE v_u L946 <- DMA wv<-in_moe_w_val_dram: 0.4, 1, 0.4
```

The exponential is 1.75 us earlier, `g_u0_0` only 0.65 (30.89), later than I expected; PE then waits 0.4 us for the weights. The time lies between the two ranges set, and its interval overlaps that of the small pattern alone, so what the move adds is not clear of the noise.

## Why the prediction was right and wrong

The time, 293.79 us and 292.64 in the second series, is inside the range (286.5 to 295.5) and 1.7 to 2.9 us above the forecast of 290.9. In part that is luck: the start of `g_u0_0` in the base was 2.1 us too late, and the 35.0 forecast for it was too late as well, by 2.0 or 0.2 us. One of the signs that the prediction set against itself came true: PE idles 1.34 and 1.37 us between `g_u0_0` and its last product, more than a microsecond. Step by step:

- *"On the median, 290.24, it is 290.9."* This step failed first. The profile of before carried a fall of the clock that the median does not: 34.40 for `g_u0_0` there, 32.28 without it. The sum was made against 34.40, so `g_u0_0` at 35.0 looked like +0.6 and was +2.7. The rows of the fall were quoted, as a rival; they should have been taken off the base.
- *"So 3.9 to 8.3 us of PE"*, from 0.16 to 0.34 us a product: mis-sized. A pair costs 0.57 us, and the transposition it replaces 0.11 to 0.16. PE's work grew by 10.3 us (282.60 against 272.28), above my upper end of 8.3. I priced the product and let the transposition of half the columns go with the one it replaces; the two stand apart by 0.21 us and 0.36 us (18.87, 19.08, 19.44).
- *"all of it before `g_u0_0`, in the 11.65 idle us"*: true only through another part of the change. Of the 11.33 us without the fall of the clock, 7.50 lie ahead of the first matmul, while `ident` is not made, and could take nothing. Alone, the products add 12.3 us to the head. In the changed kernel PE's idle time in the head falls from 11.33 to 2.56 us, and so covers 8.8 of the 9.5 us of work added there. The early start, *"worth nothing by itself"*, gives 5.6 us of that cover. The two parts had to be costed together.
- *"`wg0` is issued at 15.8, not 19.23"*: it was 19.30. I followed POOL's queue but not `hk1_u1_3`'s input: `kt_u1_3` comes from a product, late in PE's full queue, and POOL waited 3.86 us for it. So the weights did not meet the loads, and `kfT_2` came late through PE's queue, not through `kf0_2`. That it came at 25.82, near the landing forecast for 26.1, is chance.
- *Two queues*: "do not bring them earlier as a whole" and ACT held but not decisive were right in effect (head loads on SP). ACT was held to 13.61, not 16.5, and its *"floor by ACT alone"* of 33.3 us was no floor: with ACT free at 2 us the head ends at 33.39. The Trainium skill, "DMA: Bandwidth & Descriptors", section "Issuing engines are not separate DMA queues", has transfers of several engines share the 16 engines; the trace agrees, 33.39 against 33.03 us. What the queues do change is which load stands behind which: 6 us for `v_0_1`.
- *"The stretch between has no idle time to win; a new order can shift it by a microsecond"*: +0.80 of work and +0.85 of idle time, where I had +0.6. And I missed that the stretch holds a floor of its own: of the two us gained at `g_u0_0` by dropping spare products, 1.6 went there.
- *The tail*, -0.5: measured -0.4.

Shown, then: the products' work and that it is uncovered without the other parts; that PE sets the head's end (spare products); that ACT's transfers do not; that PE's waits between 68 and 104 swallow most of a shorter head. The loss itself is 2.0 us between like executions (head, work and waits behind it, less the tail), and 1.8 more in the execution with the late pace. No one part was shown to cause it: undoing the products, the queue, or the order behind gives 291.7 to 292.5 us each. What PE waits for between 68 and 104 was not settled: the traces name v in one run and k_2 in others. A kernel with both the old order behind and the lighter head was not run.
